# An instruction order made with longer assumed transfers and vector work and later attention matmuls, in a fused attention and maxout kernel

## The chip, the core and the metric

The kernel runs on one core of a Trainium2 chip. A core has a matmul engine (TensorE, PE here), three vector engines (VectorE or DVE, ScalarE or ACT, GpSimd or POOL) and SyncE (SP), which issues all of this kernel's DMAs. Each engine takes its instructions in the order in which the program has them; between engines they wait on semaphores. The metric is the time of one execution on the device, in microseconds, median of three runs.

## What is computed

Attention of two kinds is added, and the sum goes through a two-layer maxout block. Batch 8, heads 8, sequence 576, head width 64; the block has 4608 tokens, width 512, inner width 768. All is float32.

```python
q_d = q.reshape(B, H, Sd, factor, D).mean(axis=3)      # factor 4: 144 pooled positions
...
out_d = sm_attn(q_d, k_d, v_d)                         # softmax attention on pooled q, k, v
out_up = np.repeat(out_d, factor, axis=2)
mask = np.abs(pos[:, None] - pos[None, :]) < factor    # a band of 7 positions
...
out_local = np.matmul(attn, v)                         # softmax attention inside the band
attn_out = out_up + out_local
x = attn_out.transpose(0, 2, 1, 3).reshape(B * S, H * D)
h = np.maximum(np.maximum(x @ w1, x @ w2), x @ w3)
return h @ w_out
```

## The kernel before

**Numbering.** The code counts batches j from 0 to 8. Batches 0 to 7 hold the first 512 positions of each sequence; batch 8 holds the last 64 of all eight sequences. Attention is done by half-batches of four heads, n = 2j and 2j + 1, so n runs from 0 to 17. Half-batches 0 to 3 (`DENSE`) compute the band as matmuls. From n = 4 on the band goes another way: the window scores (`pa<-qk`) are copied to `sm`, stored to DRAM (`scr`), and read back as seven numbers per position (`s`); after the softmax on DVE and ACT, the seven products with `v` are made by ACT, POOL or DVE into `pvb` and added by DVE into `x`. `turned` then transposes `x` in blocks of 32 on DVE and finishes the transposition by a strided store to DRAM (`xd`).

**The pooled chain.** For each half-batch up to n = 15, PE makes the pooled scores (`pa<-qkT`); DVE reduces the maximum, ACT takes the exp into `pd`, DVE or ACT scales it by `rd`, DVE transposes it in blocks (`pd<-pd`), SP stores it to DRAM (`pdd<-pd`, `pdd<-pdt`) and loads it back transposed (`pt<-pdd`, `ptt<-pdd`), and PE makes the pooled values (`pa<-pt,vd` and `pa<-ptt,vtail`). ACT copies these to `od`. The PSUM tag `pa` has four banks that are given out in the program's order, so the pooled scores of n + 1 come behind the pooled values of n.

**The layers.** `transposes` loads `xd` back as `xs`, adds `od`, and splits the sum into `xhi` and `xlo` (chunks 0 to 3; the first half-batch makes chunks 0 and 1, the second 2 and 3). `mlp_in` needs 216 matmuls of 128x512 for a batch (six blocks of inner width, three weights, four chunks, three products each), `mlp_out` 72. These 288 are called layer matmuls below. Their results are taken from PSUM by ACT (`t<-pm`, `hh_0r`, `y`) and DVE (`t<-pm,t`, `hh_1r`). After 18 matmuls of `mlp_out` a `y` is stored to the output by SP.

**What sets the order.** Nothing is issued when the Python code calls it. A `Recorder` collects every operation with the operations that it needs, and `place` (lines 233 to 366) plays the program forward with assumed costs: at each step the engine and the operation that can start first are taken, by priority where several can. What comes out is one fixed order per engine, and where an operation may run on several engines, its engine too. An operation counts as ready `lag` ns behind the end of what it needs; `LAG` is 600 for attention. PE operations of attention have priority over the layers' wherever they count as ready. The times of this play are assumptions; on the chip each engine keeps the order and waits for what is really late.

**Buffers.** The planner also gives out the buffers of each tag in turn: `x` has five (`XBUFS`), shared by `x`, its transposed copy `xt`, and early window loads of `v`; `v` has two.

## Time and profile before

| | |
|---|---|
| median of three runs | 773.93 us (772.67 to 776.02) |
| the profiled execution | 776.07 us, span from first to last instruction 774.3 us |
| mean granted TensorE clock | 0.970 |
| chain that ended last | PE 42%, DVE 23%, DMA 16%, SP 7%, ACT 6% |
| layer matmuls | 2592 |
| DMA queue share of 16 engines | 52.4% |

How to read the rows: a group is `line engine operation output<-inputs`, with buffer numbers left out; nearly all instructions carry line 410, that of the function that records them, so tiles tell them apart. In a row of waits stand the total in us, the number of waits and the longest. In a timeline row stand start and duration in us, then engine and operation; in brackets is the idle time ahead of it and what ended it. PE's matmuls overlap, so a busy share of PE is not a share of its peak.

### The profile page before, as it was taken

Reading aid. Unit: us, or ns where it says so; the run is one execution under the profiler, and the core shown is the slowest. Engines: PE = TensorE matmul, PEld = TensorE weight load, DVE = VectorE, ACT = ScalarE, POOL = GpSimd, SP = SyncE. Lnnn points to the kernel's source line nnn. Section 1 sums busy time; section 2 is a strip of 40 time slices with the busy share of each in tenths; the row PEclk is TensorE's granted clock in tenths of the full one; section 3 lists DMA queues with packets and bytes.
Section 4 is the critical chain, followed back from the end, with each engine's and each line's share of the span. In section 5 each row is a group of like instructions: output and inputs, shape, how many; then the busy total and the mean of one; then the engine's idle time right before and its main releaser. Section 6 shows DMA issues by size and latency. Waiting matters only on the chain.

```text
span 774.3 us, 13146 instructions
## 1 busy us (share of the span) xinstructions
PE 706.7 (91%) x4544; PEld 562.9 (73%) x4544; DVE 532.7 (69%) x1008; ACT 389.0 (50%) x1331; POOL 187.0 (24%) x273
## 2 busy tenths in 40 slices
PE   3578999999998999899897989899999999999997
PEld 2456777787776777677686867686778888888885
DVE  6999998658988869699774968579677432241220
ACT  5665555346774667467282639377386321121111
POOL 0002000036443353226153313166064100000000
PEclk9869999999999999999899989999999999999999
DMA  8935323763787665886775657785763220011002
GB/s 284 352 101 195 113 90 115 194 135 95 139 248 172 138 147 119 237 154 153 150 179 105 110 141 183 166 145 131 151 153 80 57 68 14 14 56 41 1 0 55
DMA packets 189600, 100.29 MB, mean 130 GB/s; under 512 B 161262, under 2 KB 165389, under 8 KB 188765
## 3 DMA queue, kind: packets, MB, share of 16 engines
q1 hardware_dynamic: 189533, 99.44, 52.4%
q8 instruction: 36, 0.59, 0.3%
q14 instruction: 31, 0.25, 0.1%
HBM read 70.18 MB, written 29.23 MB: 128 GB/s over the span
## 4 chain that ended last, share of the span: by engine, by line
PE 42%; DVE 23%; DMA 16%; SPq 7%; ACT 6%; issue 4%; POOL 3%; DVEq 0%; ACTq 0%; POOLq 0%
PE pm L410 37%; SPq L410 7%; DVE pvb L410 6%; PE pa L410 5%; ACT pvb L410 3%; DVE t L410 3%; POOL pvb L410 3%; DMA s<-scr 2%; DMA ptt<-pdd 2%; DMA v<-in_v_dram 2%; DMA x<-in_vw_dram 2%; DVE x L410 2%; DMA scr<-sm 2%; DVE sm L410 1%; DVE xlo_0r L410 1%
## 5 line engine op out<-in xcount | busy, mean ns | idle before, releaser
L410 PE MATMUL pm<-xlo_0r,whi_0r 128*128 128x512 f32 x648 | 255.7, 395 | 1.6 <-DVE xlo_0r L410 1.6
L410 PE MATMUL pm<-xhi_0r,wlo_0r 128*128 128x512 f32 x648 | 255.1, 394 | 0.7 <-DVE wlo_0r L410 0.7
L410 PE MATMUL pm<-xhi_0r,whi_0r 128*128 128x512 f32 x648 | 254.0, 393 | 1.3 <-DVE t L410 1.3
L410 POOL TENSOR_TENSOR pvb<-v,s 128x256 f32<-128x256 f32 x214 | 155.4, 759 | 184.5 <-DVE s L410 85.6
L410 ACT ACTIVATE pvb<-v,s 128x64 f32<-128x64 f32 x712 | 179.0, 340 | 39.9 <-DMA v<-in_v_dram 24.6
L410 DVE TENSOR_TENSOR t<-pm,t 128x512 f32<-128x512 f32 x108 | 73.9, 684 | 114.6 <-PE pm L410 111.7
L410 PEld LDWEIGHTS pm<-xlo_0r,whi_0r 128*128 128x128 f32 x648 | 122.3, 189 | 28.9 <-DVE xlo_0r L410 2.3
L410 PEld LDWEIGHTS pm<-xhi_0r,wlo_0r 128*128 128x128 f32 x648 | 122.6, 189 | 27.6 <-issue 1.6
L410 PEld LDWEIGHTS pm<-xhi_0r,whi_0r 128*128 128x128 f32 x648 | 122.3, 189 | 27.5 <-DVE t L410 1.5
L410 DVE TENSOR_TENSOR pvb<-pvb 128x768 f32<-128x768 f32 x112 | 103.5, 924 | 19.7 <-ACT pvb L410 12.3
L410 ACT CAST hh_0r<-t 128x512 fp32r<-128x512 f32 x54 | 33.4, 619 | 118.9 <-DVE t L410 118.7
L410 PE MATMUL pm<-wo_0r,hh_1r 128*128 128x512 f32 x216 | 84.9, 394 | 2.7 <-DVE hh_1r L410 2.7
L410 PE MATMUL pm<-wo_0r,hh_0r 128*128 128x512 f32 x216 | 85.0, 394 | 1.7 <-ACT hh_0r L410 1.3
L410 PE MATMUL pm<-wo_1r,hh_0r 128*128 128x512 f32 x216 | 85.9, 397 | 0.1
L410 ACT COPY y<-pm 128x512 f32<-128x512 f32 (+1 forms) x44 | 25.6, 586 | 64.7 <-PE pm L410 60.8
L410 PEld LDWEIGHTS pm<-wo_0r,hh_1r 128*128 128x128 f32 x216 | 40.8, 189 | 12.0 <-DVE hh_1r L410 4.0
L410 PEld LDWEIGHTS pm<-wo_0r,hh_0r 128*128 128x128 f32 x216 | 40.8, 189 | 11.2 <-ACT hh_0r L410 2.0
L410 ACT COPY t<-pm 128x512 f32<-128x512 f32 x54 | 31.4, 582 | 34.1 <-PE pm L410 34.0
L410 PEld LDWEIGHTS pm<-wo_1r,hh_0r 128*128 128x128 f32 x216 | 40.9, 189 | 9.8 <-issue 0.9
L410 DVE TENSOR_TENSOR hh_1r<-t,hh_0r 128x512 fp32r<-128x512 f32 x54 | 38.6, 716 | 11.4 <-ACT hh_0r L410 11.0
L410 PEld LDWEIGHTS pa<-qk 64*64 64x64 f32 x1024 | 20.6, 138 | 20.5 <-ACT pd L410 9.4
L410 PE MATMUL pa<-qk 64*64 64x70 f32 x1024 | 26.4, 234 | 8.4 <-ACT pd L410 7.4
(122 smaller groups left out, 706.2 us busy)
## 6 DMA issues: line engine op xcount, KB each, us to landing
qk<-in_qk_dram SPq DMA_DIRECT2D x32, 582.0 KB
v<-in_v_dram SPq DMA_DIRECT2D x55, 320.0 KB
out_dram<-y SPq DMA_DIRECT2D x36, 256.0 KB
scr<-sm SPq DMA_DIRECT2D x56, 140.0 KB
xd<-x SPq DMA_DIRECT2D x112, 64.0 KB
t<-xd SPq DMA_DIRECT2D x28, 256.0 KB
wo<-in_wi_dram SPq DMA_DIRECT2D x4, 1536.0 KB
pdd<-pd SPq DMA_DIRECT2D x48, 80.0 KB
```

The source lines that it names most:

```text
L410: getattr(self.engines[o.eng], method)(*map(real, args), **{k: real(x) for k, x in kw.items()})
```

## The change

Three numbers of the planner are new, and apply to the attention of half-batches 4 to 17. A PE operation there counts as ready 2500 ns behind what it needs (`PELAG`) and not 600. What needs a transfer counts as ready at least 2000 ns behind its end (`DMA_LAG`). Work of these half-batches on all engines but PE is assumed to take 1.15 times as long (`SLOW`). `LAG` stays where these aren't set.

The buffers change as well. `v` has three buffers and not two. `x` is transposed in place, so no second `x` buffer is taken for it. To make room, `ident` and `bandmask` lie in one of the five `x` buffers until their last use at n = 3, the sums of the pooled tail are made in place in `traw`, and `ptl` and `ptd` share columns that neither needs from the other.

```diff
+VBUFS = 3
 LAG = 600.0
+PELAG = 2500.0
+DMA_LAG = 2000.0
+SLOW = 1.15
...
-        o.lag = self.lag
+        o.dlag = 0.0 if self.pelag == self.lag else DMA_LAG
+        o.lag = self.lag if "PE" not in forms else self.pelag
...
-                assert info["k"] + bufs >= len(order), ("used after its buffer was given on", info["name"])
+                assert info["k"] == 0 or info["k"] + bufs >= len(order), ("used after its buffer was given on", info["name"])
...
-                o.cost[e] = (sum(x[0] for x in c) + turn, any(x[1] for x in c))
+                o.cost[e] = ((sum(x[0] for x in c) + turn) * (1.0 if e == "PE" or not o.dlag else SLOW), any(x[1] for x in c))
...
-                u.ready = max(u.ready, free[e] if same else o.end + u.lag)
+                u.ready = max(u.ready, free[e] if same else o.end + max(u.lag, u.dlag if e == "SP" else 0.0))
...
-    ident = new([P, P], name="ident")
+    consts = new([P, P + FAC * KWIN], tag="x", bufs=XBUFS, name="consts")
+    ident, bandmask = consts[:, :P], consts[:, P:].rearrange("p (u x) -> p u x", u=FAC)
...
-    ptd = new([P, P], name="ptd")
-    ptl = new([P, P], name="ptl")
+    ptld = new([P, P + N64], name="ptld")
+    ptl, ptd = ptld[:, :P], ptld[:, N64:]
...
-        h = new([N64, 2 * D], tag="th", name=f"th_{n}")
+        h = raw[:, : 2 * D]
...
-            act.copy(ptt, pst2[:, P:])
+            act.copy(ptt[:N64], pst2[:N64, P:])
...
-            vv = new([P, HW], tag="v", bufs=2, name=f"v_{n}_{g}")
+            vv = new([P, HW], tag="v", bufs=VBUFS, name=f"v_{n}_{g}")
...
-        t = new([P, FAC, P], tag="x", bufs=XBUFS, name=f"xt_{j}_{c}")
-        dve.transpose(out=t, in_=x)
+        t = x
+        dve.transpose(out=t, in_=t)
...
-            with at(100.0 * n + 100.0, LAG):
+            with at(100.0 * n + 100.0, LAG, PELAG):
                 begin(n + 1)
...
-            with at(100.0 * n, LAG):
+            with at(100.0 * n, LAG, LAG if n in DENSE else PELAG):
                 attention(n)
```

**What moves at n = 15.** On PE the pooled values of n = 15 stand before inside the second layer of batch 5 (`wo` and `hh` are its operands), 1693 layer matmuls into the program:

```order
L410 MATMUL pm_3_166<-wo_0r_1108,hh_1r_712 128x512
L410 MATMUL pm_2_164<-wo_0r_1108,hh_0r_701 128x512
L410 MATMUL pa_1_199<-pt_0_339,vd_1_439 64x144 x2
L410 MATMUL pa_1_199<-ptt_0_109,vtail1_0_99 64x144 x2
L410 MATMUL pa_2_203<-qk_1_121 64x70
```

In the changed order they stand inside the first layer of batch 6 (`xlo`, `whi4`), 1892 in:

```order
L415 MATMUL pm_2_161<-xhi2_0r_79,whi4_0r_85 128x512
L415 MATMUL pm_2_161<-xlo2_0r_81,whi4_0r_85 128x512
L415 MATMUL pa_1_196<-pt_0_335,vd_1_456 64x144 x2
L415 MATMUL pa_1_196<-ptt_0_107,vtail1_0_99 64x144 x2
L415 MATMUL pa_2_200<-qk_1_118 64x70
```

So 199 more layer matmuls stand ahead of the last pooled values, and 199 fewer behind them. On DVE the block transposition of `pd` of n = 15 stands before behind the eviction of layer matmul 1620 (the row of `t_2<-pm_0` just ahead):

```order
L410 TENSOR_TENSOR x_1_125<-pvb_0_272 128x4x64
L410 TENSOR_TENSOR t_2_615<-pm_0_138,t_2_615 128x512
L410 STREAM_TRANSPOSE pd_0_91<-pd_0_91 128x640
L410 TENSOR_TENSOR hh_1r_712<-t_2_615,hh_0r_701 128x512
L410 TENSOR_SCALAR pdt_0_101<-pdt_0_101,rd_0_269 64x144
L410 STREAM_TRANSPOSE pdt_0_101<-pdt_0_101 64x160
```

Now it stands behind the eviction of layer matmul 1800, and `x` beside it is turned in place:

```order
L415 TENSOR_TENSOR x_0_93<-pvb_0_268 128x4x64
L415 TENSOR_TENSOR t_1_403<-pm_2_161,t_1_403 128x512
L415 STREAM_TRANSPOSE pd_0_91<-pd_0_91 128x640
L415 STREAM_TRANSPOSE x_0_93<-x_0_93 128x512
L415 COPY sm_1_190<-pa_3_303 128x280
L415 TENSOR_TENSOR hh_1r_719<-t_1_403,hh_0r_705 128x512
```

Between that eviction and the pooled values lay 73 layer matmuls, and lie 92 now.

**What moves where batch 2 enters the first layer.** On PE the layer began before with one PSUM bank filled through all chunks of `x`, the pooled values of n = 5 standing 38 layer matmuls ahead of it:

```order
L410 MATMUL pm_0_138<-xhi0_0r_71,whi0_0r_69 128x512
L410 MATMUL pm_0_138<-xlo0_0r_73,whi0_0r_69 128x512
L410 MATMUL pm_0_138<-xhi0_0r_71,wlo0_0r_70 128x512
L410 MATMUL pm_0_138<-xhi1_0r_72,whi0_0r_69 128x512
L410 MATMUL pm_0_138<-xlo1_0r_74,whi0_0r_69 128x512
L410 MATMUL pm_0_138<-xhi1_0r_72,wlo0_0r_70 128x512
L410 MATMUL pm_0_138<-xhi2_0r_79,whi0_0r_69 128x512
L410 MATMUL pm_0_138<-xlo2_0r_81,whi0_0r_69 128x512
```

Now the pooled values stand behind the layer's first matmul, three banks are filled with chunks 0 and 1 and a fourth is begun before `xhi2` is used; the window scores of n = 6 follow at once:

```order
L415 MATMUL pm_3_163<-xhi1_0r_73,whi0_0r_69 128x512
L415 MATMUL pm_3_163<-xlo1_0r_74,whi0_0r_69 128x512
L415 MATMUL pm_3_163<-xhi1_0r_73,wlo0_0r_70 128x512
L415 MATMUL pm_1_137<-xhi0_0r_71,whi1_0r_75 128x512
L415 MATMUL pm_1_137<-xlo0_0r_72,whi1_0r_75 128x512
L415 MATMUL pm_1_137<-xhi0_0r_71,wlo1_0r_76 128x512
L415 MATMUL pm_0_135<-xhi2_0r_79,whi0_0r_69 128x512
L415 MATMUL pa_1_196<-qk_2_159 64x70
```

Chunk 2 is used 21 matmuls into the layer and no longer 6. On SP the loads of `pt` and `ptt` of n = 5 stood ahead of the output stores of batch 1, and the load of the last chunk (`t_0<-xd_3`) behind the second of them:

```order
L410 DMA s_0_1466<-scr_0_1344 128x16x7
L410 DMA pt_0_339<-pdd_1_1953 128x576
L410 DMA ptt_0_109<-pdd_1_1953 32x1x144 x2
L410 DMA v_1_135<-in_v_dram 128x640
L410 DMA qk_0_119<-in_qk_dram 128x1164
L410 DMA t_1_396<-xd_2_2005 128x512
L410 DMA out_0_dram<-y_0_264 128x512
L410 DMA xd_3_2063<-x_3_129 128x4x32 x4
L410 DMA qk_1_121<-in_qk_dram 128x1164
L410 DMA traw_0_131<-in_v_dram 64x1x256
L410 DMA out_0_dram<-y_1_266 128x512
L410 DMA t_0_393<-xd_3_2063 128x512
```

Now `pt` and `ptt` stand behind the second output store and the last chunk's load (`t_1<-xd_3`) behind the fourth:

```order
L415 DMA out_0_dram<-y_0_260 128x512
L415 DMA t_0_390<-xd_2_1999 128x512
L415 DMA v_1_132<-in_v_dram 128x640
L415 DMA out_0_dram<-y_1_262 128x512
L415 DMA pt_0_335<-pdd_1_1958 128x576
L415 DMA ptt_0_107<-pdd_1_1958 32x1x144 x2
L415 DMA xd_3_2096<-x_3_124 128x4x32 x3
L415 DMA out_0_dram<-y_0_260 128x512
L415 DMA xd_3_2096<-x_3_124 128x4x32
L415 DMA qk_1_118<-in_qk_dram 128x1164
L415 DMA out_0_dram<-y_1_262 128x512
L415 DMA t_1_403<-xd_3_2096 128x512
```

An output store waits for its `y`, and so for the 18 matmuls of the second layer that make it; what stands behind it on SP waits too.

More of the change, by code (lines that the diff above doesn't have):

```diff
@@ L123, in __init__ @@
         self.ops, self.tags, self.of, self.masks = [], {}, {}, {}
-        self.prio, self.lag, self.run = 0.0, 0.0, None
+        self.prio, self.lag, self.pelag, self.run = 0.0, 0.0, 0.0, None
         self.engines = {"PE": nc.tensor, "DVE": nc.vector, "ACT": nc.scalar, "POOL": nc.gpsimd, "SP": nc.sync}
@@ L442, in at @@
     @contextmanager
-    def at(prio, lag=0.0):
-        was = rec.prio, rec.lag
-        rec.prio, rec.lag = prio, lag
+    def at(prio, lag=0.0, pelag=None):
+        was = rec.prio, rec.lag, rec.pelag
+        rec.prio, rec.lag, rec.pelag = prio, lag, lag if pelag is None else pelag
         yield
-        rec.prio, rec.lag = was
+        rec.prio, rec.lag, rec.pelag = was
     @contextmanager
@@ L477, in local_global_attention_maxout_kernel @@
     ptt = new([P, SD], name="ptt")
-    ptd = new([P, P], name="ptd")
-    ptl = new([P, P], name="ptl")
+    ptld = new([P, P + N64], name="ptld")
+    ptl, ptd = ptld[:, :P], ptld[:, N64:]
     nm = new([P, 5], name="nm")
     zd = new([P, 5], name="zd")
-    bandmask = new([P, FAC, KWIN], name="bandmask")
     pvb = new([P, 2 * NO * FAC * D], name="pvb")
@@ L515, in load_constants @@
     def load_constants():
-        for t in (*qtail, *vtail, pdt, ptd, ptl, ptt, nm, zd):
+        for t in (*qtail, *vtail, pdt, ptld, ptt, nm, zd):
             dve.memset(t, 0.0)
@@ L749, in band_load @@
             else:
-                t = new([P, HW], tag="v", bufs=2, name=f"vwin_{n}_{g}")[:KWIN, : SEG // QT * D].rearrange("p (t d) -> p t d", d=D)
+                t = new([P, HW], tag="v", bufs=VBUFS, name=f"vwin_{n}_{g}")[:KWIN, : SEG // QT * D].rearrange("p (t d) -> p t d", d=D)
             sp.dma_start(t, vw_d[n // 2, HH * (n % 2) + g])
@@ L806, in band_pooled_values @@
         for g in range(0, HH, 2):
-            vv = new([P, 2, FAC * D], tag="v", bufs=2, name=f"v_{n}_{g}")
+            vv = new([P, 2, FAC * D], tag="v", bufs=VBUFS, name=f"v_{n}_{g}")
             sp.dma_start(vv, dram(v, (j * H + h0 + g) * S * D, [[FAC * D, P], [S * D, 2], [1, FAC * D]]))
@@ L918, in block @@
         for n in (2 * j, 2 * j + 1):
-            with at(100.0 * n, LAG):
+            with at(100.0 * n, LAG, LAG if n in DENSE else PELAG):
                 attention(n)
         if DENSE and 2 * j + 1 == DENSE[-1]:
-            with at(100.0 * n + 100.0, LAG):
+            with at(100.0 * n + 100.0, LAG, PELAG):
                 begin(n + 1)
```

## The prediction

> **What bounds the kernel now.** I read the page's busy times and slices first, then TensorE's waits, then the timeline at those waits.
>
> ```profile
> PE 706.7 (91%) x4544; PEld 562.9 (73%) x4544; DVE 532.7 (69%) x1008; ACT 389.0 (50%) x1331; POOL 187.0 (24%) x273
> ```
>
> TensorE (PE) is busy 91% of the 774.3 us; nothing else comes near. So the end is the sum of PE's own work and of the time in which PE stands. The table by stage says where it stands:
>
> ```profile
> 0.00:140.00 140.00, 107.94 (x984) 84.75 (x984) 127.41 (x241) 81.18 (x254) 8.89 (x19) 0.93 0.53 175
> 140.00:600.00 460.00, 429.98 (x2824) 338.75 (x2818) 359.76 (x701) 274.73 (x1014) 175.79 (x250) 0.97 0.68 152
> 600.00:774.30 174.30, 168.76 (x745) 139.42 (x743) 45.49 (x68) 33.14 (x63) 2.36 (x4) 1.00 0.12 34
> ```
>
> The columns are the stretch, then PE, weight loads, DVE, ACT and POOL busy, the granted clock, and DMA. PE lacks 32.1 us before 140, 30.0 us between 140 and 600, and 5.5 us in the tail. In the first stage VectorE is busy 127.4 of 140 us with the weight split, so PE waits there for DVE. After 140 no other engine is full (DVE 78%), so those 30.0 us are waits for single results. PE's waits name them:
>
> ```profile
> PE pa L410 <- DMA pt<-pdd: 9.9, 7, 2.9
> PE pa L410 <- ACT pd L410: 7.4, 6, 2.8
> PE pa L410 <- DMA ptt<-pdd: 7.1, 7, 2.3
> PE pm L410 <- DVE hh_1r L410: 2.7, 3, 1.6
> PE pm L410 <- ACT hh_0r L410: 1.3, 1, 1.3
> PE pa L410 <- DMA qk<-in_qk_dram: 0.9, 1, 0.9
> ```
>
> These six rows make 29.3 of the 30.0 us. The pooled values (`pa<-pt,vd`, `pa<-ptt,vtail`) wait for the transposed probabilities on their way through DRAM: 9.9 + 7.1 = **17.0 us**. The window scores wait 7.4 us for a PSUM bank that ACT's exp still reads. PE works in order, so the layer matmuls behind such a wait stand too, ready or not. That they are ready shows in the end of the chain of waits:
>
> ```profile
> 566.13 202.65 PE pm L410 x893
> ```
>
> From 566 us on PE does nothing but layer matmuls, 202.65 / 893 = **0.2269 us** each. That is 3.1 batches of 288, with almost all of attention done. Attention therefore needs no speed; it only must not hold PE up.
>
> Here are three of those waits, and a place without one:
>
> ```profile
> 246.29 0.47 PE L410 MATMUL pa<-pt,vd 128*64 128x144 f32 x4 [1.00 <-DMA pt<-pdd]
> 247.26 0.47 PE L410 MATMUL pa<-ptt,vtail 128*64 128x144 f32 x4 [0.51 <-DMA ptt<-pdd]
> ...
> 419.22 0.47 PE L410 MATMUL pa<-pt,vd 128*64 128x144 f32 x4 [2.87 <-DMA pt<-pdd]
> 420.79 0.59 PE L410 MATMUL pa<-ptt,vtail 128*64 128x144 f32 x4 [1.10 <-DMA ptt<-pdd]
> ...
> 422.27 1.33 PE L410 MATMUL pa<-qkT 64*128 64x144 f32 x8
> ...
> 525.33 0.76 PE L410 MATMUL pa<-qkT 64*128 64x144 f32 x8
> ...
> 560.43 0.47 PE L410 MATMUL pa<-pt,vd 128*64 128x144 f32 x4 [0.95 <-DMA pt<-pdd]
> 562.29 0.47 PE L410 MATMUL pa<-ptt,vtail 128*64 128x144 f32 x4 [1.40 <-DMA ptt<-pdd]
> ```
>
> The wait has a second price. The eight matmuls on `qkT` take 0.76 us at 525, behind no wait, and 1.33 us at 422, behind 2.87 + 1.10 us of waiting. The table in steps of 2 us and of 20 us shows why:
>
> ```profile
> 418.00:420.00 2.00, 0.47 (x4) 0.23 (x4) 0.99 (x5) 0.30 (x1) 0.00 (x0) 1.00 0.81 236
> 422.00:424.00 2.00, 2.00 (x16) 1.17 (x12) 0.00 (x0) 2.00 (x9) 1.96 (x4) 0.50 0.04 10
> ...
> 380.00:400.00 20.00, 19.36 (x148) 14.86 (x145) 13.77 (x34) 12.52 (x49) 7.98 (x12) 0.83 0.55 152
> 420.00:440.00 20.00, 19.21 (x150) 15.00 (x151) 14.39 (x30) 13.71 (x55) 8.67 (x15) 0.91 0.54 88
> 440.00:460.00 20.00, 16.68 (x78) 12.51 (x77) 14.82 (x31) 4.67 (x17) 2.42 (x4) 0.83 0.69 162
> ```
>
> The granted clock falls to 0.50 behind the wait. The three 20 us stretches with waits for `pt` and `ptt` at 380, 420 and 450 lack (0.17 + 0.09 + 0.17) x 20 = 8.6 us of full clock.
>
> [...]
>
> **The change, part by part.** *The planner's assumptions* (`PELAG`, `DMA_LAG`, `SLOW`). They remove no instruction; they move them. The order shows how far. Between the pooled values of consecutive half-batches (n = 4 to 15) stood 99, 99, 127, 111, 103, 118, 127, 98, 125, 125, 122 layer matmuls, 114.0 on average; now 136, 104, 143, 134, 138, 124, 161, 122, 138, 133, 118, or 131.9. That is 17.9 x 0.2269 = 4.1 us more cover per half-batch, against a mean wait of 17.0 / 12 = 1.4 us. At n = 15 the chain itself is seen:
>
> ```profile
> 544.50 0.83 DVE L410 STREAM_TRANSPOSE pd<-pd 128x640 f32<-128x640 f32 x1
> ```
>
> From the transposition at 544.50 to the start on `ptt` at 562.29 pass 17.8 us of DMA issue and landing. Before, 73 layer matmuls (16.6 us) stand on PE behind the last eviction ahead of that transposition; now 92 (20.9 us). The 4.3 us more exceed the 0.95 + 1.40 us of the wait. The largest wait, 3.97 us at n = 11, has its interval grow by 34 matmuls, 7.7 us. Three intervals grow by little or shrink: n = 6 by 5 (1.1 us against a wait of 1.51), n = 10 by 6 (1.4 us against about 1.5), n = 15 by -4 in all. I leave 0.4 + 0.1 + 3.3, about 4 us, of the 17.0: **-13 us** (bounds: -17.0 if none is left, -5 if most of the cover is eaten by a later chain).
>
> *The clock behind those waits*, 8.6 us at most. Part of it falls into time in which PE waits anyway, so I take half: **-4 us** (0 to -8.6).
>
> *The window scores' wait for ACT*, 7.4 us. Between pooled scores and window scores stood 24.5 layer matmuls on average, now 27.5. Of the six intervals that wait, four grow (by 7, 11, 14 and 3), one stays and one shrinks by 10. **-1.5 us** (+2 to -7.4). The waits for `hh_1r`, `hh_0r` and `qk` (4.9 us) are evictions and a load to which the change does nothing direct: 0.
>
> *What is late next.* Later attention feeds the layers later. The pooled values of n = 5 stand now behind the first matmul of batch 2's first layer, where they stood 38 matmuls ahead of that layer. `xhi2` and `xlo3` of that batch need them. Before:
>
> ```profile
> 217.63 0.47 PE L410 MATMUL pa<-pt,vd 128*64 128x144 f32 x4
> 234.08 0.50 PE L410 MATMUL pm<-xlo_0r,whi_0r 128*128 128x512 f32 x1 [0.53 <-DVE xlo_0r L410]
> ```
>
> The last `xlo` came 16.5 us after the pooled values began. In the new order PE has 29 layer matmuls (6.6 us) before `xhi3`, 10 more before `xlo3` (2.3 us), and about 3.6 us of pooled values, scores and window scores between: 12.5 us. If the 16.5 repeat, PE stands 4 us. On SP the load of `xs` for the last chunk stands now behind the fourth output store, where it stood behind the second, so it can start only when the second layer of batch 1 is done:
>
> ```profile
> 224.93 3.15 DMA t<-xd
> ```
>
> With the copy of `y`, this load, the add, the cast and the subtraction (0.6 to 0.75 us each by their groups) that makes about 6 us, and PE would not stand at all. Between 0 and 4 I take **+2 us** (0 to +6). The loads of `pt` and `ptt` of n = 5 also moved on SP, from ahead of the first output store to behind the second:
>
> ```profile
> 556.23 1.41 SPq L410 DMA_DIRECT2D pt<-pdd x1
> ```
>
> At n = 15 it is 6.1 us from there to PE's start on `ptt`; at n = 5 PE has 37 matmuls, 8.4 us, less 0.6 for the copy of `y`: no wait. At the later batches the pooled values stand 41, 57, 60, 88 and 125 matmuls ahead of the layer, 9.3 us and more: 0.
>
> *Buffers.* The constants hold one of five `x` buffers until n = 3. The window loads of n = 1 are behind n = 0's release in both orders:
>
> ```profile
> 22.29 7.46 SPq L410 DMA_DIRECT2D x<-in_vw_dram x3
> 46.30 0.47 PE L410 MATMUL pm<-y,x 70*64 70x64 f32 x2 [1.85 <-ACT y L410]
> ```
>
> Three of four are issued from 22.29 to 29.75 and used at 46.30, behind ACT. A fourth issued with them is hidden by 16 us: 0 (0 to +3, if the first use slips past ACT's copy). The third `v` buffer and the transposition in place ease SP and the pools. Muls move between engines by 2 or 3%: ACT 712 to 732 instructions, POOL 214 to 209. All of that lies beside PE's work: 0 (-2 to +2).
>
> **The sum:** -13 - 4 - 1.5 + 2 = **-16.5 us**. The profiled execution took 776.07 us (span 774.3 and 1.8 around it), so it would take 759.6; it stands 2.1 us over the median of the three runs, 773.93, so the median would be **757.4**.
>
> A second way to the same number: from 185.3 us (pooled values of n = 4) to 560.4 (n = 15) PE does 1254 layer matmuls, 284.5 us, in 375.1. Of the 90.6 left, 28 are waits, so about 62 are attention's own matmuls and slow clock. Now 1451 matmuls stand there, 329.2 us: with 58 of attention that is 387 without any wait, 35.2 a half-batch, where the chain through softmax and DRAM went at 34.1. The pace that PE's order sets and the pace that the chain showed are nearly equal. That is why I expect most waits to go and not all.
>
> **The rivals.** *The waits stay by half.* SP issues the stores and loads of the chain in order, and the stores of one half-batch take long:
>
> ```profile
> 548.78 1.26 SPq L410 DMA_DIRECT2D pdd<-pd x2
> 550.13 2.31 SPq L410 DMA_DIRECT2D pdd<-pdt x4
> 552.54 2.89 SPq L410 DMA_DIRECT2D xd<-x x4
> ```
>
> If SP is what makes the chain late, 8.5 us of the 17.0 come back, and the clock and ACT's wait with them: -8.5 - 1 + 3 = -6.5, a median of 767. For it: these rows are 6.5 us in a row. Against: the cover grows by 4.1 us a half-batch, three times the mean wait. Chance 0.20.
>
> *All of it goes*: -17.0 - 8.6 - 7.4 = -33, a median of 741. Against: three intervals did not grow. Chance 0.10.
>
> *The chain itself becomes the bound; slower.* The end follows from the pace P of a half-batch: 185.3 + 11 P, then the 700 layer matmuls left behind n = 15 (158.8 us) and 9.9 us of other work, as now (774.3 - 560.4 - 899 x 0.2269), and 1.8 around: 355.8 + 11 P. Today P is 34.1; the forecast of 759.6 has P = 36.7. Over 780 (0.5% above 776) it takes P above 38.6. The assumed delays add 2 x 1.9 us (two steps to PE) and 2 x 1.4 us (two DMA steps) to a half-batch's chain. If 4.5 of these 6.6 us turn into real waiting, because every queue now takes the chain's steps later, the kernel is slower; with all of them P is 40.7 and the median about 801. Against: the mean interval is 131.9 matmuls and not over 144, so attention still gains on the layers by the order. Chance 0.08.
>
> **How the numbers follow.** Forecast 0.62 (749 to 763), half the waits 0.20 (763 to 773), all gone 0.10 (below 749), slower 0.08. The range takes the case with half the waits up to 770 and the one with none down to 743; about 0.2 is left out. A measurement of this kernel can tell about 0.5% from no change, so faster is below 770: 0.62 + 0.10 + three quarters of 0.20, less 0.03 for mishaps at the start, 0.84. Within 0.5%: 0.08. Slower: 0.08.
>
> **What would show it.** Right: `pt` and `ptt` together under 6 us in PE's waits; no 20 us stretch between 380 and 460 below a clock of 0.9; the last run of layer matmuls begins at about 700 left and not 893. The step on batch 2 shows as a wait of PE for `xhi` or `xlo` near 230 us, under 6 us. Wrong: waits for `xhi` or `xlo` at batches 3 to 5, or PE's idle time before 140 us above 35, or waits for `pt` above 8 us.

## The result and the profile after

The changed kernel takes **735.46 us** (median of 4 runs, 733.52 to 741.36) against 773.93 us (772.67 to 776.02) for the kernel before: a ratio of **0.9515 [0.9466, 0.9564]**. The forecast was 757.4 us with a range from 743 to 770, so it had the sign right and less than half of the gain. The profiled execution is the longest of the four, 741.36 us with a span of 739.5.

The busy times of the changed kernel, and its table by stage (columns as in the prediction):

```profile
PE 698.1 (94%) x4544; PEld 559.7 (76%) x4544; DVE 523.3 (71%) x1002; ACT 396.3 (54%) x1359; POOL 175.0 (24%) x265
```

```profile
0.00:140.00 140.00, 111.16 (x990) 86.95 (x992) 124.50 (x238) 84.25 (x264) 7.97 (x18) 0.93 0.53 177
140.00:600.00 460.00, 452.91 (x2970) 361.99 (x2967) 354.91 (x699) 277.18 (x1005) 156.97 (x232) 0.99 0.66 152
600.00:739.50 139.50, 134.04 (x592) 110.75 (x590) 43.90 (x68) 34.92 (x91) 10.03 (x15) 0.99 0.15 39
```

TensorE's idle time falls from 32.1 to 28.8 us in the first stage and from 30.0 to 7.1 between 140 and 600; in the tail it stays at 5.5. Its busy time falls from 706.7 to 698.1. These three, 3.2 + 22.9 + 8.6, and 0.1 in the tail are the 34.8 us between the two spans. The instructions are the same 4544 matmuls, so the 8.6 us of busy time are not work left out: they are matmuls that ran slower before, at a granted clock of 0.97 in the middle stage where it is 0.99 now. The traces' record of the granted clock agrees: between 140 and 600 us it has 0.50 for 23.9 us before (from 195.71, 380.03, 420.99, 451.71 and 533.63 us on) and for 6.8 us now (from 393.00 and 539.78 on), which is 11.9 and 3.4 us of full clock lost.

The waits of TensorE between 140 and 600, of the changed kernel (total us, times, longest):

```profile
PE pa L415 <- DMA pt<-pdd: 3.2, 3, 1.8
PE pa L415 <- DMA ptt<-pdd: 2.0, 2, 1.8
PE pa L415 <- ACT pd L415: 0.8, 1, 0.8
PE pa L415 <- ACT pdt L415: 0.6, 1, 0.6
PE pm L415 <- ACT hh_0r L415: 0.5, 1, 0.5
```

Not only the waits for `pt` and `ptt` went (17.0 to 5.2 us), but also those on ACT's exponentials (7.4 to 1.4) and on the evictions of the hidden layer (4.0 to 0.5). Of the last two the forecast had left nearly all in place.

The end of the chain of waits of the changed kernel:

```profile
576.03 158.01 PE pm L415 x696
```

The run of layer matmuls that nothing interrupts is 696 long, as the forecast had it (about 700, before 893).

### The profile page after: what moved, and what is told of

It reads as the page before. It is cut to its first block, busy times and chain, and to the rows that moved or that the text cites. A ratio compares the mean times of both kernels' runs of the same rounds, so it can differ in the third digit from the quotient of the medians.

```text
span 739.5 us, 13101 instructions
## 1 busy us (share of the span) xinstructions
PE 698.1 (94%) x4544; PEld 559.7 (76%) x4544; DVE 523.3 (71%) x1002; ACT 396.3 (54%) x1359; POOL 175.0 (24%) x265
## 4 chain that ended last, share of the span: by engine, by line
PE 72%; DVE 11%; DMA 10%; SPq 3%; issue 2%; ACT 2%; DVEq 0%; ACTq 0%
PE pm L415 65%; PE pa L415 6%; SPq L415 3%; DMA traw<-in_v_dram 3%; DVE pvb L415 2%; DMA qk<-in_qk_dram 2%; DVE wo L415 2%; DVE t L415 2%; DMA ptt<-pdd 1%; DVE sm L415 1%; DMA out_dram<-y 1%; DMA x<-in_vw_dram 1%; DMA pt<-pdd 1%; ACT pvb L415 1%; DMA pvb<-in_wo_dram 1%
## 5 line engine op out<-in xcount | busy, mean ns | idle before, releaser
L415 POOL TENSOR_TENSOR pvb<-v,s 128x256 f32<-128x256 f32 x209 | 147.0, 734 | 192.8 <-DVE s L415 61.7
L415 ACT ACTIVATE pvb<-v,s 128x64 f32<-128x64 f32 x732 | 184.7, 340 | 9.7 <-DVE s L415 5.1
L415 PEld LDWEIGHTS pm<-xhi_0r,whi_0r 128*128 128x128 f32 x648 | 121.9, 188 | 26.4 <-issue 1.1
L415 PEld LDWEIGHTS pm<-xhi_0r,wlo_0r 128*128 128x128 f32 x648 | 121.9, 188 | 25.6 <-issue 0.6
L415 DVE TENSOR_TENSOR pvb<-pvb 128x768 f32<-128x768 f32 x112 | 99.0, 884 | 10.9 <-POOL pvb L415 8.7
L415 PE MATMUL pm<-wo_0r,hh_0r 128*128 128x512 f32 x216 | 83.2, 393 | 1.4 <-ACT wo_0r L415 0.9
L415 ACT CAST xhi_0r<-t 128x512 fp32r<-128x512 f32 x32 | 19.5, 617 | 16.7 <-DVE t L415 12.6
L415 PEld LDWEIGHTS pa<-qk 64*64 64x64 f32 x1024 | 18.9, 133 | 12.1 <-issue 4.4
```

Source lines behind the costliest of these rows:

```text
L415: getattr(self.engines[o.eng], method)(*map(real, args), **{k: real(x) for k, x in kw.items()})
```

## The experiments

Two theories stood first. Theory A is the prediction's own: what counts is how many layer matmuls TensorE has between two pooled values. Theory B: the buffers do it. After the first four runs theory C took their place: what counts is that the vector engines' work, and SyncE's, is planned with the time that it takes on the chip. Each ratio below is against runs of the kernel before on the same chip, with its 95% interval. Three planner numbers occur: `PELAG` (wait of a matmul behind what it needs, 2500 ns), `DMA_LAG` (wait behind a transfer, 2000 ns) and `SLOW` (factor 1.15 on the price of whatever the attention of half-batches 4 to 17 does off TensorE, SyncE's issues included; the layers' matmuls keep their price in every run, and their evictions and the split into `xhi` and `xlo` in every run but e12). 600.5 for `PELAG` means: as before, with the other two left in force, since the code turns them off where `PELAG` equals `LAG`. In these runs the kernel before took medians of 767.8 to 771.5 us (762.85 to 777.29 in single executions) and not 773.93. So the forecasts of e1 to e4, made from 773.93, are to be read as ratios, and spans of profiles from different runs can differ by some us without any change of the kernel.

### Which part of the change

**e1, the buffers alone** (all three numbers off):

```diff
-PELAG = 2500.0
+PELAG = 600.0
```

> The changed kernel with its new buffers, but with the old planner numbers (no later matmuls, no longer transfers, no slower vector work). Pooled values are 112.6 layer matmuls apart on average, as before (114.0). Theory A (the gain is the cover on TensorE): 768 to 778 us, TensorE waits 12 to 20 us for pt and ptt, and its idle time between 140 and 600 us stays near 30 us. Theory B (the third v buffer and the transposition in place keep DVE, ACT and SP on time): 755 us or less, idle time between 140 and 600 us under 18 us.

Measured: 763.61 us, ratio 0.9927 [0.9889, 0.9966]. **e2, the numbers alone**, is the kernel before with these lines and the code that uses them, on the old tiles:

```diff
+PELAG = 2500.0
+DMA_LAG = 2000.0
+SLOW = 1.15
```

> The old kernel with its old buffers (two v, a second x buffer for the transposed copy) and the three new planner numbers. Pooled values are 136.2 layer matmuls apart, more than in the changed kernel (131.9), but five batches (2 to 6) enter the first layer with chunks 2 and 3 late by order. Theory A: 733 to 745 us, waits for xhi and xlo under 5 us in all. Theory B: attention can't keep up with two v buffers, so TensorE waits 10 us or more for xhi and xlo, and the time is 750 us or more.

Measured: 736.09 us, 0.9596 [0.9543, 0.9649]. Theory B falls: the gain is in the planner's numbers, and the buffers bring less than 1%, if anything, beside them. As ratios e1 and e2 lie in theory A's ranges. What the numbers start from on the new buffers is seen in e1's waits between 140 and 600:

```profile
PE pa L415 <- DMA pt<-pdd: 9.7, 7, 2.1
PE pa L415 <- DMA ptt<-pdd: 7.1, 9, 1.7
PE pa L415 <- DVE z L415: 2.4, 1, 2.4
PE pm L415 <- DVE hh_1r L415: 2.2, 4, 0.6
PE pa L415 <- ACT pd L415: 0.5, 1, 0.5
```

The waits for `pt` and `ptt` are those of the kernel before (16.8 us against 17.0), but ACT's exponentials hold TensorE for 0.5 us and not for 7.4, with the old planner numbers still in force. So how much TensorE waits for exponentials differs from order to order, and that it fell in the changed kernel does not by itself show what the numbers do.

**e3, later matmuls alone**, and **e4, all but later matmuls** (behind a transfer a matmul still waits 2000 ns there):

```diff
 PELAG = 2500.0
-DMA_LAG = 2000.0
-SLOW = 1.15
+DMA_LAG = 600.0
+SLOW = 1.0
```

> The changed kernel with the later attention matmuls alone (transfers at 600 ns, vector work at 1.0). Pooled values are 120.2 layer matmuls apart, a third of the way from 114.0 to 131.9. Theory A: a third to a half of the gain, 752 to 764 us, with 7 to 13 us of waits for pt and ptt. Rival (it is the 1.9 us at TensorE itself that counts, since that is where the wait was): 735 to 743 us.

```diff
-PELAG = 2500.0
+PELAG = 600.5
```

> The changed kernel without the later attention matmuls (600 ns; behind a transfer 2000), with longer transfers and vector work at 1.15. Pooled values are 126.6 layer matmuls apart, 70% of the way. Theory A: 740 to 752 us, with 4 to 8 us of waits for pt and ptt. Rival (the later matmuls do it): 760 us or more.

Measured: e3 763.93 us, 0.9953 [0.9921, 0.9984]; e4 737.44 us, 0.9613 [0.9555, 0.9671]. Later matmuls add cover (120.2 against e1's 112.6) and bring nothing beside e1's 0.9927; without them the gain is whole or nearly so, since the intervals of e4 and of the whole change touch. As ratios e4 lies in theory A's range and e3 outside it: it was to have a third to a half of the gain. Why e3 gains nothing is seen in its waits between 140 and 600:

```profile
PE pa L415 <- ACT pd L415: 9.3, 8, 3.0
PE pa L415 <- DMA pt<-pdd: 4.6, 3, 2.7
PE pm L415 <- DVE hh_1r L415: 2.9, 3, 1.6
PE pm L415 <- ACT hh_0r L415: 1.8, 2, 1.5
PE pa L415 <- DMA ptt<-pdd: 1.5, 3, 0.5
```

`pt` and `ptt` are down to 6.1 us from 17.0, as cover should do; but TensorE stands 14.0 us for ACT's exponentials and for the hidden layer, where it stood 11.4 before and 2.7 in e1.

### Which of the numbers

**e5, the prices alone; e6, the wait behind transfers alone; e7, far later matmuls alone; e8, prices too high:**

```diff
-PELAG = 2500.0
-DMA_LAG = 2000.0
+PELAG = 600.5
+DMA_LAG = 600.0
 SLOW = 1.15
```

> The changed kernel with only the factor 1.15 on vector work left: matmuls wait 600.5 ns in the plan instead of 2500, transfers 600 ns instead of 2000; new buffers kept. Layer matmuls between pooled values: 121.9 on average (before 114.0, e3 120.2, e4 126.6). Theory A (what counts is the amount of layer work between one pooled value and the next): hardly more than e3, 755 to 764 us, 12 to 20 us of idle PE between 140 and 600. Theory C (what counts is that the vector engines' work is planned with the time that it takes, so that evictions and exponentials come out in the order in which they are needed): 735 to 745, waits for ACT's exp and for hh under 2 us together, while waits for pt and ptt may stay at 4 to 8 us.

```diff
-PELAG = 2500.0
-SLOW = 1.15
+PELAG = 600.5
+SLOW = 1.0
```

> The changed kernel with only the 2000 ns behind a transfer left: matmuls wait 600.5 ns behind vector work, vector work at factor 1.0. Layer matmuls between pooled values: 129.7 on average. Theory A (amount of layer work): as the whole change, 734 to 745, waits for pt and ptt under 4 us. Theory C (vector work planned with its time): most of the gain stays away, 752 to 764, with waits of PE for exponentials and hidden values of 6 us and more.

```diff
-PELAG = 2500.0
-DMA_LAG = 2000.0
-SLOW = 1.15
+PELAG = 4500.0
+DMA_LAG = 600.0
+SLOW = 1.0
```

> As e3 (later matmuls alone), but with 4500 ns in place of 2500: the layer work between pooled values grows from 120.2 to 130.7 matmuls, about that of the whole change (131.9), while transfers and vector work are planned as before. Theory A: 734 to 745 us, waits for pt and ptt under 4 us. Theory C, or a theory in which the transfers' own time must be planned: 750 to 764, with pt and ptt again at 4 us or more, or waits for exponentials as in e3 (9.3).

```diff
-SLOW = 1.15
+SLOW = 1.3
```

> The changed kernel with a factor 1.3 in place of 1.15 on vector work: 144.2 layer matmuls between pooled values, more than half a batch of layers has (144), so the layers run out of finished attention: the pooled values of batches 2 to 8 stand right ahead of the matmuls that need them. My rival in the prediction (the chain becomes the bound) prices this at 355.8 + 11 P; with P = 144.2 x 0.2269 + 5 = 37.7 that is 771 if the tail is as before; by the shorter tail of the changed kernel (its pooled values ended at 572 of 739.5) and one wait of 1 to 4 us at each of seven batches I expect 740 to 760. Theory A without that starvation: 733 to 737.

Measured: e5 739.63 us, 0.9591 [0.9556, 0.9627]; e6 758.94, 0.9882 [0.9810, 0.9955]; e7 755.52, 0.9806 [0.9781, 0.9831]; e8 752.12, 0.9756 [0.9728, 0.9784]. **Theory A falls here.** e5 has 121.9 layer matmuls between pooled values and nearly the whole gain; e6 with 129.7 and e7 with 130.7, as many as the changed kernel, have a quarter and two fifths of it. e7's waits show what A missed:

```profile
PE pa L415 <- ACT pd L415: 8.0, 6, 2.8
PE pm L415 <- DVE hh_1r L415: 2.9, 3, 1.2
PE pm L415 <- ACT hh_0r L415: 1.8, 2, 1.0
```

The view has no row for `pt` or `ptt` any more, which is what the cover was to do, and TensorE still loses 12.7 us to results of VectorE and ScalarE that come late. e6 gains as little as theory C had it, but not for the reason given: its waits are for the probabilities.

```profile
PE pa L415 <- DMA pt<-pdd: 13.1, 9, 3.1
```

In e5 the waits for ACT and the hidden layer are nearly gone, and those for `pt` and `ptt` are a third of what they were, in e1 as in the kernel before:

```profile
PE pa L415 <- DMA pt<-pdd: 3.1, 2, 2.6
PE pa L415 <- DMA ptt<-pdd: 2.8, 4, 1.3
PE pm L415 <- DVE hh_1r L415: 1.1, 2, 0.7
PE pa L415 <- ACT pd L415: 1.1, 2, 0.7
```

Beside e1, from which it differs by `SLOW` alone, TensorE's idle time in this stage falls from 22.1 to 8.2 us, and its busy time in all from 706.3 to 695.6.

e8 shows the other side, where attention comes too late for the layers:

```profile
PE pm L415 <- ACT xhi_0r L415: 5.7, 5, 1.9
PE pm L415 <- DVE xlo_0r L415: 3.6, 3, 1.7
```

These are the waits for `xhi` and `xlo` that the prediction named as the sign of starvation. The kernel is still faster than before, since all the other waits are gone.

### Why the prices matter

The planner of this kernel makes a timetable of all engines and then writes each engine's instructions in that order. The chip keeps the order, not the times. The prices stand in `price`: 62 + 1.045 ns an element for an add on VectorE, 140 + 1.68 ns for a multiplication on GpSimd, 530 ns for the issue of a transfer. The groups of the kernel before, between 140 and 600 us (busy us, mean ns of one), and the issues of the chain's first store (minimum, median and maximum in ns):

```profile
L410 POOL TENSOR_TENSOR pvb<-v,s 128x256 f32<-128x256 f32 x210 | 153.1, 762 | 177.2 <-DVE s L410 85.6 <-DMA v<-in_v_dram 33.5 <-DVE x L410 19.4
...
L410 DVE TENSOR_TENSOR pvb<-pvb 128x768 f32<-128x768 f32 x55 | 58.2, 1058 | 14.3 <-ACT pvb L410 9.1 <-POOL pvb L410 5.1
...
L410 DVE TENSOR_TENSOR pvb<-pvb 128x512 f32<-128x512 f32 x55 | 43.7, 794 | 2.2
```

```profile
L410 SPq DMA_DIRECT2D pdd<-pd x48: 569/640/3552, 161.3 to 549.4; - x48
```

The plan has 570, 865, 597 and 530 ns for these four. Neighbours on VectorE overlap by some 80 ns, so I also added up what each of its instructions holds the engine for, from its start to the next one's where they follow closely: 369.5 us between 140 and 600, where the plan's prices for the same instructions give 296.0. That is 25% more; SyncE's issues come to 311.0 us against 235.8, or 32% more.

What this does is seen at n = 5 in the kernel before. `qkT` makes the pooled scores, `nm` is their maximum, `pd<-pa,nm` the exponential, `pa<-qk` the window scores, which need a bank that the exponential still reads:

```profile
186.44 0.76 PE L410 MATMUL pa<-qkT 64*128 64x144 f32 x8
186.97 0.43 DVE L410 TENSOR_TENSOR x<-pvb 128x256 f32<-128x256 f32 x1
187.43 0.71 DVE L410 STREAM_TRANSPOSE x<-x 128x512 f32<-128x512 f32 x1
188.06 0.65 DVE L410 TENSOR_TENSOR t<-pm,t 128x512 f32<-128x512 f32 x1
...
189.51 0.69 DVE L410 TENSOR_TENSOR hh_1r<-t,hh_0r 128x512 fp32r<-128x512 f32 x1
190.11 1.02 DVE L410 TENSOR_REDUCE nm<-pa 128x2 f32<-128x288 f32 x3
...
191.75 1.06 ACT L410 ACTIVATE pvb<-v,s 128x64 f32<-128x64 f32 x4
...
194.14 0.37 ACT L410 ACTIVATE pd<-pa,nm 128x144 f32<-128x144 f32 x1
...
195.02 0.71 PE L410 MATMUL pa<-qk 64*64 64x70 f32 x30 [2.78 <-ACT pd L410]
```

Nothing on VectorE waits between 186.97 and 190.11: it is simply still busy with what stands ahead of the maximum. `nm` is done at 191.33 (its last row, left out here), and ScalarE has another 2.8 us of other work ahead of the exponential. The plan has 1.8 us from the scores to the maximum and 4.0 to the exponential; the chip takes 3.7 and 7.7. TensorE reaches the window scores by a plan that was made with 4.0, and stands 2.78 us. This is the old plan's widest miss at this step; on average over n = 4 to 15 it plans 5.5 us from the scores to the exponential, and the chip takes 6.8. The changed kernel plans 6.1 on average and takes 6.1; at n = 5 it plans 5.6 us and takes 5.4:

```profile
187.50 0.76 PE L415 MATMUL pa<-qkT 64*128 64x144 f32 x8
190.33 1.02 DVE L415 TENSOR_REDUCE nm<-pa 128x2 f32<-128x288 f32 x3
192.92 0.36 ACT L415 ACTIVATE pd<-pa,nm 128x144 f32<-128x144 f32 x1
194.45 0.72 PE L415 MATMUL pa<-qk 64*64 64x70 f32 x32
```

Over all of attention it adds up. From the pooled scores of n = 4 to those of n = 15 the kernel before plans 338.5 us and takes 381.1 by its trace (144.21 here to 525.33 in the prediction's row); the changed kernel plans 386.1 and takes 397.1:

```profile
144.21 0.76 PE L410 MATMUL pa<-qkT 64*128 64x144 f32 x8
```

```profile
143.34 0.76 PE L415 MATMUL pa<-qkT 64*128 64x144 f32 x8
540.45 1.33 PE L415 MATMUL pa<-qkT 64*128 64x144 f32 x8
```

The table has this for every kernel: the stretch by its own plan, by its trace, how far the chip falls behind, the end of the whole plan, and the span (all us; the last eight stand below).

```
                     plan   chip   late  plan's end  span
before               338.5  381.1  42.6  718.0  774.3
e1 buffers           330.9  363.5  32.6  717.1  762.0
e3 PELAG 2500        347.5  376.4  28.9  717.1  758.5
e6 DMA_LAG           377.8  404.0  26.3  717.6  757.2
e7 PELAG 4500        378.5  400.8  22.4  717.1  753.4
e5 SLOW 1.15         358.8  370.6  11.7  717.1  738.9
changed              386.1  397.1  11.0  718.7  739.5
e4 DMA_LAG, SLOW     372.7  382.4   9.7  718.5  735.7
e2 old buffers       408.8  413.8   5.0  721.3  734.3
e8 SLOW 1.3          432.3  436.3   4.0  739.6  750.7
e9 SyncE             328.8  358.9  30.0  717.1  755.4
e10 VectorE          359.8  379.9  20.2  717.1  744.9
e11 calibrated       379.9  386.8   7.0  717.1  733.3
e13 SLOW 1.08        344.5  369.9  25.4  717.1  757.2
e14 SLOW 1.25        388.0  395.6   7.6  718.1  734.8
e15 TensorE 0.87     322.0  352.0  30.0  711.4  752.7
e16 e11 and waits    379.6  387.4   7.8  717.1  735.4
e12 all batches      399.9  402.6   2.7  744.6  746.1
```

In all but e12 the span is the plan's end, plus the lateness in this stretch, plus 7 to 15 us (in e12, whose first batches are planned with other prices too, less 1). The plan's own pace for attention hardly matters (e5 plans 358.8 and e2 408.8, and both are fast); that the chip keeps to it does. A slow plan is not enough for that: e6 and e7 plan 378 us and fall 22 to 26 us behind, where e4, e11 and e16, with 373 to 380 us planned, fall 7 to 10 behind. What sets these three apart is `SLOW`. e8 is on time and slow, because its plan ends 21 us later. Lateness contains TensorE's waits, so this is bookkeeping, not yet a cause; the next runs vary the prices one by one.

### Whose price, and how much

**e9, SyncE alone; e10, VectorE alone; e11, a factor for each engine as measured; e12, the same for all batches.** `SLOW` becomes a table by engine:

```diff
-SLOW = 1.15
+SLOW = {"SP": 1.15}
...
-                o.cost[e] = ((sum(x[0] for x in c) + turn) * (1.0 if e == "PE" or not o.dlag else SLOW), any(x[1] for x in c))
+                o.cost[e] = ((sum(x[0] for x in c) + turn) * (1.0 if not o.dlag else SLOW.get(e, 1.0)), any(x[1] for x in c))
```

with `PELAG` at 600.5 and `DMA_LAG` at 600 in all of them.

> The factor 1.15 on the issue of transfers on SyncE alone (530 to 609.5 ns each in the plan); vector work at 1.0, no longer waits for matmuls or behind transfers; new buffers. Layer matmuls between pooled values: 114.4 on average, as before. If e5's gain came from pricing the chain's stores on SyncE: 735 to 745 us, waits for pt and ptt under 6 us. If it came from pricing the vector engines (theory C): 758 to 766 us, about as e1, with 14 us and more of waits for pt and ptt.

```diff
-SLOW = {"SP": 1.15}
+SLOW = {"DVE": 1.15}
```

> The factor 1.15 on VectorE alone; ScalarE, GpSimd and SyncE at 1.0, everything else as in e9. Layer matmuls between pooled values: 123.5 on average. Theory C in its narrow form (VectorE is the one that is priced too low: its instructions from 140 to 600 us hold it for 369.5 us in the trace of before, where the plan's own prices for the same instructions add up to 296.0): 738 to 748 us. If all of the non-TensorE prices are needed: 750 to 762 us.

```diff
-SLOW = {"SP": 1.15}
+SLOW = {"DVE": 1.25, "POOL": 1.26, "SP": 1.32, "ACT": 1.03}
```

> In place of one factor 1.15, a factor for each engine from what the trace of before shows against the plan's prices: VectorE 1.25, GpSimd 1.26, SyncE 1.32, ScalarE 1.03; no longer waits for matmuls, none behind transfers. Layer matmuls between pooled values: 131.2 on average. Theory C: at least as good as e5, 730 to 740 us, PE idle between 140 and 600 under 8 us. If e5's gain was luck of one order rather than the right prices: anything from 740 to 760.

```diff
-                o.cost[e] = ((sum(x[0] for x in c) + turn) * (1.0 if not o.dlag else SLOW.get(e, 1.0)), any(x[1] for x in c))
+                o.cost[e] = ((sum(x[0] for x in c) + turn) * SLOW.get(e, 1.0), any(x[1] for x in c))
```

> As e11, with the same prices for the other batches too (in the changed kernel they hold only for the attention of batches 3 to 9 and what is planned with it, so the first 140 us are planned with the old ones). Layer matmuls between pooled values: 137.3 on average. Theory C: the first 140 us lose less than 28.8 us of PE time (25 or less) and the time is 725 to 738. Rival: the start is bound by VectorE's own work (127 of 140 us busy there), so that no order of it helps: 28 to 32 us lost there, time as e11 or up to 8 us above it.

Measured: e9 756.26 us, 0.9791 [0.9741, 0.9841]; e10 750.95, 0.9737 [0.9678, 0.9797]; e11 735.63, 0.9524 [0.9474, 0.9573]; e12 747.04, 0.9678 [0.9632, 0.9724]. Beside e1's 0.9927 SyncE's price alone brings 1.4% and VectorE's 1.9%; e5, which has both and those of ScalarE and GpSimd, brings 3.4%. The two add up to 3.3%, but each interval is half a percent wide to either side, and ScalarE and GpSimd were not run alone. So no engine does it alone: both narrow readings fall, e10's at the lower edge of the range given for "all prices are needed", and e9 2 us under the range that theory C gave it. The measured factors of e11 give the whole gain with no longer wait at all.

e12's own forecast fell: priced so, the middle is nearly perfect, and the start worse than in any other kernel here.

```profile
0.00:140.00 140.00, 100.60 (x858) 78.34 (x858) 114.36 (x213) 76.54 (x249) 8.75 (x22) 0.88 0.49 166
140.00:600.00 460.00, 458.29 (x3070) 367.11 (x3068) 351.56 (x693) 304.76 (x1109) 140.77 (x218) 1.00 0.66 153
```

TensorE lacks 39.4 us before 140 and 1.7 behind it. Its plan ends at 744.6 us already, and the chip keeps it to 746.1: the plan is worse to begin with. (What its forecast calls batches 3 to 9 are 2 to 8 in this document's count.) The factors are those of 140 to 600 us, and they are not right for the start. Added up in the same way over the first 140 us of the kernel before, VectorE's instructions hold it for 130.0 us against 118.4 planned, or 10% more, and SyncE's issues take 28.6 us against 31.3. So e12 prices the start too high. That this is all of its loss is not shown.

**e13 and e14, the factor 1.08 and 1.25 alone; e15, TensorE cheaper instead** (these three, like e10 and e11, as edits of e9)**; e16, e11 with smaller waits** (an edit of e11)**:**

```diff
-SLOW = {"SP": 1.15}
+SLOW = {"DVE": 1.08, "POOL": 1.08, "SP": 1.08, "ACT": 1.08}
```

> As e5 (prices of the vector engines and SyncE alone), factor 1.08 in place of 1.15. Layer matmuls between pooled values: 119.2. With factor 1.0 (e1) the ratio to before was 0.993, with 1.15 (e5) 0.959. Theory C: between them, ratio 0.970 to 0.985, 745 to 759 us. If e5 was one lucky order: no gain over e1, ratio over 0.987.

```diff
-SLOW = {"SP": 1.15}
+SLOW = {"DVE": 1.25, "POOL": 1.25, "SP": 1.25, "ACT": 1.25}
```

> As e5, factor 1.25, which is VectorE's measured excess over the plan (369.5 against 296.0). Layer matmuls between pooled values: 131.7. Theory C: as good as e5 or e11, ratio 0.950 to 0.962, with PE idle between 140 and 600 under 8 us, and some starvation of batch 2 or 3 (waits for xhi or xlo up to 4 us). If e5 was one lucky order: ratio 0.965 or more.

```diff
-SLOW = {"SP": 1.15}
+SLOW = {"PE": 0.87}
```

> Prices of the vector engines and SyncE at 1.0, the price of TensorE's work in the same part times 0.87 = 1 / 1.15, everything else as in e1. Layer matmuls between pooled values: 111.2, no more than before. If only the ratio of the prices counts (the plan must not lay attention's steps out faster, in units of PE's work, than the chip does): the gain of e5, ratio 0.955 to 0.970. If the vector engines' own time must be right against the lags, transfers and each other, or if the amount of layer work counts: as e1, ratio 0.985 or more.

```diff
-PELAG = 600.5
-DMA_LAG = 600.0
+PELAG = 1500.0
+DMA_LAG = 1000.0
 SLOW = {"DVE": 1.25, "POOL": 1.26, "SP": 1.32, "ACT": 1.03}
```

> The prices of e11 (VectorE 1.25, GpSimd 1.26, SyncE 1.32, ScalarE 1.03) with smaller waits beside them: matmuls 1500 ns, transfers 1000 ns. Layer matmuls between pooled values: 134.2; batch 2 is a little starved by the order. A candidate for the best: 730 to 737 us, PE idle between 140 and 600 under 5 us. If prices and waits together overshoot as e8 did: 738 to 750, with waits for xhi and xlo of 3 us or more.

Measured: e13 756.82 us, 0.9822 [0.9773, 0.9872]; e14 733.91, 0.9524 [0.9481, 0.9567]; e15 758.77, 0.9857 [0.9802, 0.9911]; e16 735.14, 0.9542 [0.9505, 0.9579]. The response to the factor is steady: 0.9927 at 1.0, 0.9822 at 1.08, 0.9591 at 1.15, 0.9524 at 1.25. So e5 was no lucky order.

e15 does not decide whether only the ratio to TensorE's price counts. Its factor reaches the TensorE work of half-batches 4 to 17 alone, 44.4 of the 674.6 us that the plan of the kernel before has for TensorE; the 2592 layer matmuls stay at 231 ns each, so attention is not planned slower against them. What e15 shows is that cheaper attention matmuls bring no more than e1 has. A run with cheaper layer matmuls is missing, and one with longer waits behind VectorE, ScalarE and GpSimd in place of prices. So it stays open whether the prices have to be right, or whether attention only has to be planned slower on all these engines at once. e14, whose 1.25 for ScalarE is far from the measured 1.03, is as good as e11.

Beside these prices longer waits add nothing that can be seen (e16 against e11; at 1.15, e4 against e5, while the whole change lies 0.8% below e5 with intervals that overlap at the edge), and the changed kernel, e2, e11, e14 and e16 end at the same 0.95 to 0.96. No version beats the change by more than can be measured: what is left is the start (28 us or more of idle TensorE in each) and the tail.

## Why the prediction was right in sign and short by half

By its own steps, in us of the two profiled executions:

- **What bounds the kernel**: right. TensorE's idle time in the middle was the thing to win, attention's speed was not, and the last run of layer matmuls came out at 696.
- **`pt` and `ptt`, -13**: they fell by 11.8, from 17.0 to 5.2. The size was right, and e7 shows that cover can remove them; that cover explains the size is not shown, since e6 has as much of it (129.7 matmuls) and still waits 13.8 us, and e5 waits 5.9 with 121.9. **This is the step that failed**: it read all three numbers as delays whose worth is the layer work between pooled values, and took that cover for the whole mechanism. The delays alone bring 0.9882 (e6) and 0.9806 (e7) with that cover; `SLOW` alone brings 0.9591 without it. `SLOW` makes the attention's work on the other engines longer in the plan, nearer to what the chip takes, and puts these instructions and issues at other places on every engine.
- **The window scores' wait for ACT, -1.5**: it fell by 6.0. The step counted matmuls between scores and scores again, as if the exponential were ready at a fixed time. e7 has as many such matmuls as the changed kernel, about 28 on average, and waits 8.0 us. How much of the fall is due to the numbers stays open, since e1, without them, has 0.5 us of this wait and e5 1.1; with delays alone it is back at 9.3 (e3) and 8.0 (e7).
- **`hh_1r`, `hh_0r`, `qk`, 0**: the first two fell by 3.5. "The change does nothing direct" was the wrong argument: their evictions stand in the same queues as the softmax (`hh_1r` and the maximum in the rows at n = 5), so they move with it although their own prices stay. e1 has 2.2 us of them, e5 1.1.
- **The clock, -4**: TensorE's busy time fell by 8.6. That this is the upper bound of the term is chance: the bound counted three drops of the clock and there were five, with those at 195.7 and 533.6 us, so that 11.9 us could be won, and 3.4 are still lost. The halving was wrong: time that waits might absorb was taken off, and nearly all of the clock behind the waits that went came back. In the changed kernel two waits still cost clock, those for `pt` and `ptt` of n = 10 (at 391 us) and n = 14 (at 537 us):

```profile
380.00:400.00 20.00, 17.65 (x89) 13.68 (x88) 12.01 (x28) 6.76 (x24) 7.25 (x13) 0.91 0.67 169
540.00:560.00 20.00, 20.00 (x149) 15.45 (x146) 14.88 (x29) 13.58 (x54) 11.78 (x19) 0.92 0.60 148
```

  The longest wait in the middle is 1.8 us now, and the clock still drops.
- **Starvation at batch 2, +2**: there is no such wait. The step was right about what starves and wrong about the size; in e8, whose order was to starve batches 2 to 8, it is seen at all of them but 5.
- **Buffers and start, 0**: the start gained 3.2. e1's first stage gained 3.9 with the buffers alone (TensorE busy 111.87 of 140), so this part may well be theirs; but e2, without them, gained 2.3 there, so whose it is stays open.

The differences from the forecast, 4.5 + 3.5 + 4.6 + 2 + 3.2, with 1.4 of smaller waits and less 1.2 on `pt` and `ptt`, are 18.0 of the 18.3 us between -16.5 and -34.8. The profiled run of the changed kernel lies 5.9 us over its median (before: 2.1), which adds the rest.

The three signs that the prediction named for being right all came: `pt` and `ptt` at 5.2 us together, no stretch of 20 us between 380 and 460 below 0.9, 696 layer matmuls left. They look only at the step whose size was right; none looks at the other waits, so they could not tell the forecast from the rival in which all goes.

Of the rivals, "all of it goes" (741, chance 0.10) is nearest to what happened. The argument against it, that three intervals did not grow, is theory A once more. The prediction's second way to its number fails too: it took the 34.1 us a half-batch of the kernel before for the chain's own pace, and in e15 the chip goes through the stretch above at 32.0 (352.0 / 11), against 34.6 before. The number that was missing is the old plan's pace there, 30.8 (338.5 / 11). A slower plan alone is not enough, as e6 and e7 show, which plan 34.3 and 34.4; the prices behind the plan were what to compare with the trace.

## What to carry to other kernels

Where a planner sets the order of in-order engines, compare its timetable with the trace before anything else: the step at which the chip first falls behind, and the prices of the groups on that engine, measured back to back in place. Bring the prices near to what the trace shows, in the part of the program where it was measured, and then see whether delays beside them still bring anything; one factor for all engines did as well here as one for each (e14, e11). A price that is too high lets the plan itself grow long (e8, and by its start e12). A wait that delay alone removes can come back elsewhere: e3 and e7 have less of the wait for `pt` and `ptt` than e1, and more for exponentials and evictions.

## What was not expected of the hardware

- Between 140 and 600 us VectorE's work takes 25% more than the planner's straight-line prices (369.5 us against 296.0), SyncE's issues 32% (311.0 against 235.8) and GpSimd's multiplications 34% (762 ns each against 570), with single issues of the chain's stores up to 3.55 us (row above). In the first 140 us, where GpSimd is busy for 8.9 us and not 175.8, VectorE takes only 10% more (130.0 against 118.4); why is not shown. ScalarE's multiplications come within about 7% of theirs: the 8 in this row of the kernel before take 254 ns each, against 237 planned.

```profile
189.48 2.03 ACT L410 ACTIVATE pvb<-v,s 128x64 f32<-128x64 f32 x8
```

- The granted clock of these runs goes neither by TensorE's idle time in all nor by the length of a wait alone. e15 and e1 let TensorE stand for 20.0 and 22.1 us between 140 and 600, in waits of at most 2.6 us, and were granted 1.00 and 0.97 there. In the kernel before a wait of 1.64 us leaves the clock at 1.00, and one of 1.57 us has 0.50 behind it. Here are the two, each with a stretch of 2 us behind it (the granted clock is the third number from the end):

```profile
301.11 0.50 PE L410 MATMUL pm<-wo_0r,hh_1r 128*128 128x512 f32 x1 [1.64 <-DVE hh_1r L410]
532.83 0.71 PE L410 MATMUL pa<-qk 64*64 64x70 f32 x30 [1.57 <-ACT pd L410]
```

```profile
302.00:304.00 2.00, 2.00 (x11) 1.64 (x10) 1.93 (x4) 1.71 (x7) 0.00 (x0) 1.00 0.86 205
534.00:536.00 2.00, 2.00 (x27) 1.25 (x29) 2.00 (x5) 2.00 (x10) 1.65 (x3) 0.50 0.73 168
```

  What decides between them is not shown. The same kernel is not granted the same clock each time either: e1's ten executions had means of 0.967 to 0.981.
